# Inner products of two token blocks at a time, and gate products in halves of the array, in a fused mLSTM and feed-forward kernel

## The chip, the cores and the metric

The kernel runs on one core of a Trainium2 chip. The metric is the device time of one execution in microseconds; before the change three runs took 475.63, 476.14 and 476.31 us, so the median is 476.14. The core has five engines with a queue of instructions each, which run in order and wait for one another by semaphores: TensorE (PE in the rows; PEld are its weight loads), VectorE (DVE), ScalarE (ACT), GpSimd (POOL) and SyncE (SP), which issues the DMAs.

## The reference

Three parts follow each other. First an mLSTM with a stabilised exponential gate, over 768 steps for 2 batches and 8 heads of 40 channels:

```python
m_new = np.maximum(f_gate[:, :, t] + m, i_gate[:, :, t])
f_stab = np.exp(f_gate[:, :, t] + m - m_new)
i_stab = np.exp(i_gate[:, :, t] - m_new)
C = f_stab[:, :, None, None] * C + i_stab[:, :, None, None] * np.einsum('bhd,bhe->bhde', vt, kt)
n = f_stab[:, :, None] * n + i_stab[:, :, None] * kt
h_tilde = np.einsum('bhde,bhe->bhd', C, qt)
denom = np.maximum(np.abs(nq), 1.0)
y[:, :, t] = o * h_tilde / denom
```

Its 1536 tokens of 320 channels go through a feed-forward part with 2048 inner columns and a rational function, and then through a gated one with 1536 inner columns:

```python
h = x @ w_in
P = a[0] + a[1] * h + a[2] * h2 + a[3] * h3
Q = 1.0 + np.abs(b[0]) * np.abs(h) + np.abs(b[1]) * h2
g = P / (Q + 1e-06)
x = g @ w_out
...
xn = x / rms * rms_g
silu = g * (1.0 / (1.0 + np.exp(-g)))      # g = xn @ w_gate
return (silu * val @ w_out)                # val = xn @ w_val
```

The weights come as 64-bit floats and are converted on the chip. Most products are made of 32-bit parts with a high and a low half, three products for one.

## The kernel before, in words

**Attention.** The sequence is cut into 12 chunks of 128 steps (6 for each batch). For chunk j TensorE makes the scores `s` (line 506), the forget gates' products `f` (line 486), the outputs from the state `yi` (530) and from the chunk `y` (547), and the state's update `u` (559). `f` spreads a row of gates over 128 partitions: for each head one product of a 48 x 128 selection (weights) with 128 steps; a scan on VectorE (489) turns it into decays, with which the scores are multiplied (511). `y` and `yi` are already made in halves of 64 array columns. The scan, the update and the output have steps on VectorE, GpSimd and ScalarE. The outputs of a chunk are transposed on TensorE (`xt`, 652) and split into a high part (`xh`, ScalarE, 656) and a low part (`xl`, VectorE, 660) in the tile `xall`.

**First feed-forward part.** The tokens are cut into 6 blocks of 256 (two chunks each), the inner columns into 8 pairs of 256. A unit i is one block and one pair: `PAIRS[i]` is (block, pair). Blocks 0 and 1 alternate over the pairs (units 0 to 15); then each of blocks 2 to 5 goes through all 8 pairs (units 16 to 47). A unit's inner products are tasks `in0` and `in1` (line 683): for each of two groups of 128 inner columns 8 products that move 256 tokens, into one bank of PSUM of 128 x 512. Then comes the rational function, on 128 x 512 elements: `hu`, `z`, `p1`, `h2` and `ars`, `sq` on ScalarE; `zu`, and `p2` in even units, on GpSimd; `p2` in odd units, `p3`, `w`, `y2`, `g` on VectorE (727 to 746). `g` gives the result, and tasks `out0` and `out1` multiply it by `w_out` into the accumulators of its block: units 0 to 15 in full 32-bit products (line 688), later ones in high and low parts (702, 704).

**Weights.** `c0`, `c1` (VectorE, 335 to 347), `cr`, `hi` (ScalarE) and `c2` and the last split (GpSimd, 360, 368) convert a block of weights. In0 of unit i waits for its pair of weights and for the `xl` of its block.

**Second feed-forward part.** The blocks' results are scaled, stored, loaded and transposed again; the gated products (872) and the output products (880 to 882) follow on TensorE. They fill the time from about 300 us to the end alone.

**What sets the order.** Every piece of work is a task with a number, made by `task(...)`. The table ORDER lists all 1946 numbers; `run()` (called at the end) goes through it and issues each task's instructions, and takes and gives back buffers by name (`b` are the 8 banks of PSUM). The order of instructions on each engine is thus the order in the table. These lines fix the units and the wait of the inner products:

```python
PAIRS = [(n, x - n * LAG) for x in range(NPAIR + LAG) for n in range(2) if 0 <= x - n * LAG < NPAIR]
PAIRS += [(n, p) for n in range(2, NB) for p in range(NPAIR)]
...
go("in0", lambda: inp(0), [("i", p), ("coefs",)] + ([("out0", i - 6)] if i >= 6 else []) + [("xl", 2 * n + t) for t in range(2)], ["h"])
```

## Time and profile before

| | |
|---|---|
| median of 3 runs | 476.14 us (475.63 to 476.31) |
| the profiled execution | 475.63 us, its span 473.9 us |
| TensorE busy | 457.1 us, 96% of the span, 3712 instructions |
| VectorE, ScalarE, GpSimd busy | 324.5, 307.2 and 312.2 us |
| chain that ended last | TensorE 67%, GpSimd 11%, VectorE 9%, ScalarE 8% |
| inner products, line 683 | 768 of 128 x 256, busy 104.1 us |
| forget gates' products, line 486 | 96 of 128 x 128, busy 10.1 us |

Busy times of TensorE count records whose ends are modelled: products overlap in the array, and what one costs is read from the distance between starts. The chain that ended last is followed back from the last instruction, at each step to what released it. A product of full 32-bit operands is recorded as two.

### The profile page before, as it was taken

What the parts mean: (1) busy time and instruction counts of PE and PEld (TensorE: products, weight loads), DVE (VectorE), ACT (ScalarE), POOL (GpSimd) and SP (SyncE); (2) the same over time, 40 slices, a digit from 0 to 9 for tenths busy, and PEclk for the clock granted to TensorE, in tenths of its full rate; (3) what the DMA queues carried; (4) which work ended last, traced back from release to release, by engine and by line L of the source; (5) the groups of instructions that cost most, each with busy time, mean ns of one, the idle gap of its engine ahead of it and who ended that gap; (6) DMA issues with size and microseconds to landing.
All of it is one profiled execution on the core that took longest, in us unless ns stands there. A gap on an engine that the chain in (4) does not pass through costs nothing.

```text
span 473.9 us, 9691 instructions
## 1 busy us (share of the span) xinstructions
PE 457.1 (96%) x3712; PEld 417.0 (88%) x3712; DVE 324.5 (68%) x610; ACT 307.2 (65%) x578; POOL 312.2 (66%) x326
## 2 busy tenths in 40 slices
PE   5799899999999999999999999999999999999997
PEld 4697887787889999999899888988988889999996
DVE  7899999999899999999999998972222111102201
ACT  2437999899999999999999999543131321222221
POOL 3699999999888998797797767975221431211250
PEclk9999999999999999999999999999999999999999
DMA  8797633250050104102114247422000010010001
GB/s 239 220 304 185 187 141 100 97 143 8 1 150 17 48 16 118 60 27 84 57 55 142 65 132 234 141 86 92 25 14 28 26 36 1 1 57 0 15 2 57
DMA packets 18367, 40.42 MB, mean 85 GB/s; under 512 B 3952, under 2 KB 11904, under 8 KB 18320
## 3 DMA queue, kind: packets, MB, share of 16 engines
q1 hardware_dynamic: 18320, 39.80, 27.2%
q8 instruction: 29, 0.48, 0.4%
q14 instruction: 18, 0.15, 0.1%
HBM read 35.86 MB, written 3.93 MB: 84 GB/s over the span
## 4 chain that ended last, share of the span: by engine, by line
PE 67%; POOL 11%; DVE 9%; ACT 8%; issue 3%; DMA 1%; DVEq 0%; POOLq 0%; ACTq 0%
PE bank L872 28%; PE bank L683 10%; PE bank L702 7%; PE bank L882 4%; PE bank L881 4%; PE bank L880 4%; PE bank L704 3%; POOL z L727 2%; DVE w_buf L489 2%; POOL win L368 2%; POOL vv L729 1%; POOL cv L360 1%; POOL wou L368 1%; ACT bank L739 1%; PE bank L547 1%
## 5 line engine op out<-in xcount | busy, mean ns | idle before, releaser
L683 PE MATMUL bank<-xall,win 128*128 128x256 f32 x768 | 104.1, 289 | 2.4 <-DVE xall L660 0.7
L683 PEld LDWEIGHTS bank<-xall,win 128*128 128x128 f32 x768 | 97.0, 193 | 6.6 <-DVE xall L660 1.1
L948 DVE TENSOR_TENSOR vv<-bank,vv 128x512 f32<-128x512 f32 x35 | 23.7, 688 | 69.9 <-PE bank L872 61.1
L727 POOL TENSOR_TENSOR z<-z,u 128x512 f32<-128x512 f32 x48 | 61.9, 1291 | 10.0 <-ACT z L717 9.5
L954 POOL TENSOR_TENSOR wou<-vv,wou 128x512 fp32r<-128x512 f32 x18 | 23.2, 1295 | 55.2 <-ACT wou L951 49.5
L945 ACT ACTIVATE vv<-bank 128x512 f32<-128x512 f32 x35 | 20.7, 595 | 55.1 <-PE bank L872 47.8
L756 POOL TENSOR_TENSOR gl<-vv,gh 128x512 fp32r<-128x512 f32 x32 | 41.3, 1295 | 12.9 <-issue 5.9
L872 PE MATMUL bank<-xall,w2gv 128*128 128x512 f32 (+1 forms) x256 | 46.3, 337 | 0.0
L872 PEld LDWEIGHTS bank<-xall,w2gv 128*128 128x128 f32 x256 | 39.0, 190 | 4.5
L717 ACT ACTIVATE z<-u,few 128x512 f32<-128x512 f32 x48 | 39.0, 813 | 1.0
L702 PE MATMUL bank<-wou,gh 128*128 128x320 f32 x128 | 38.6, 314 | 0.0
L704 PE MATMUL bank<-wou,gh 128*128 128x320 f32 x128 | 38.0, 309 | 0.0
L688 PE MATMUL bank<-scr,vv 128*128 128x320 f32 x128 | 37.4, 437 | 0.0
L742 DVE SCALAR_TENSOR_TENSOR z<-z,bank 128x512 f32<-128x512 f32 x48 | 32.8, 682 | 4.9 <-ACT bank L741 3.8
L335 DVE TENSOR_SCALAR bank<-raw 128x320 int32<-128x320 int32 x68 | 32.6, 487 | 4.8 <-DMA raw<-in_w_out_dram 4.2
L744 DVE SCALAR_TENSOR_TENSOR bank<-vv,few,bank 128x512 f32<-128x512 f32 x48 | 35.8, 747 | 0.0
L739 ACT ACTIVATE bank<-z,few 128x512 f32<-128x512 f32 x48 | 32.9, 685 | 2.6 <-POOL z L727 2.0
L746 DVE SCALAR_TENSOR_TENSOR vv<-z,bank 128x512 f32<-128x512 f32 x48 | 32.5, 681 | 0.7
L872 PE MATMUL bank<-win,w2gv 128*128 128x512 f32 x128 | 30.8, 391 | 0.0
L688 PEld LDWEIGHTS bank<-scr,vv 128*128 128x128 f32 x128 | 23.2, 190 | 8.4 <-issue 0.2
L716 ACT ACTIVATE u<-bank 128x512 f32<-128x512 f32 x48 | 28.5, 594 | 2.6 <-POOL z L727 1.0
L368 POOL TENSOR_TENSOR win<-cv,win 64x128 fp32r<-64x128 f32 (+2 forms) x37 | 28.0, 756 | 3.1 <-ACT win L364 1.2
(169 smaller groups left out, 1170.1 us busy)
## 6 DMA issues: line engine op xcount, KB each, us to landing
raw<-in_w_out_dram SPq DMA_DIRECT2D x14, 640.0 KB, 4.0
raw<-in_w_gv_dram SPq DMA_DIRECT2D x12, 640.0 KB, 4.1
raw<-in_w_in_dram SPq DMA_DIRECT2D x8, 640.0 KB, 5.7
lqk<-in_qk_tr_dram SPq DMA_DIRECT2D x24, 192.0 KB, 5.0
lv<-in_v_dram SPq DMA_DIRECT2D x12, 160.0 KB, 5.0
los<-in_o_gate_dram SPq DMA_DIRECT2D x12, 160.0 KB, 5.8
lk<-in_k_dram SPq DMA_DIRECT2D x12, 160.0 KB, 3.9
z_dram<-rnd SPq DMA_DIRECT2D x6, 320.0 KB, 2.3
```

What stands on the lines that cost most here:

```text
L368: POOL.tensor_tensor(out=lo, in0=v, in1=r32(hi), op=ALU.subtract)
L683: PE.matmul(out=hb()[:, e], lhsT=l, rhs=r, start=(x == 0), stop=(x == len(mm) - 1))
L688: PE.matmul(out=T("acc", n, t)[:, 0:DM], lhsT=T("vv", i)[:, e, t * 128:(t + 1) * 128], rhs=w[:, e], start=p + e == 0, stop=p == NPAIR - 1 ...
L702: PE.matmul(out=o, lhsT=l, rhs=woh[:, e], start=first, stop=last)
L704: PE.matmul(out=o, lhsT=l, rhs=wol[:, e], start=False, stop=False)
L717: go("z", lambda: ACT.activation(out=z(), in_=u(), func=ACTF.Identity, scale=babs[:, 1:2], bias=babs[:, 0:1]), [("hu", i)], ["z"])
L727: go("zu", lambda: POOL.tensor_tensor(out=z(), in0=z(), in1=u(), op=ALU.mult), [("z", i)], [], ["u"])
L739: go("ars", lambda: ACT.activation(out=hb(), in_=z(), func=ACTF.Abs_reciprocal_sqrt, bias=cq), [("zu", i), ("p3", i)])
L742: go("w", lambda: DVE.scalar_tensor_tensor(out=z(), in0=z(), scalar=1.0 + 1e-6, in1=hb(), op0=ALU.add, op1=ALU.mult), [("sq", i)])
L744: go("y2", lambda: DVE.scalar_tensor_tensor(out=hb(), in0=vv(), scalar=nacoef[:, 0:1], in1=hb(), op0=ALU.add, op1=ALU.mult), [("w", i)])
L756: go("gl", lambda: POOL.tensor_tensor(out=gl(), in0=vv(), in1=r32(gh()), op=ALU.subtract), [("gh", i)], ["gl"], ["vv"])
L872: PE.matmul(out=bank(i, e), lhsT=l, rhs=r, start=y == 0, stop=y == len(mm) - 1)
```

## The change

`NARROW = [2, 8, 8]` replaces LAG: for blocks 0 and 1 the first two pairs stay as they were (units 0 to 3). From the third pair on a unit is one group of 128 inner columns for both blocks, 512 tokens: units 4 to 15 are such wide units. Their inner products move 2 x 256 tokens in one product, so a unit has 8 products and not 16 (`in0` the first 4, `in1` the last 4), in the same bank; the polynomial has the same shapes; `out0` serves one block, `out1` the other. `in0` of a wide unit waits for the `xl` of both blocks. Blocks 2 to 5 keep their units. The forget gates' products are made as two products of 64 array columns each. ORDER is another list of the same 1946 numbers.

```diff
@@ -20,102 +20,102 @@
 OB = [["ob"] * 4, ["raw", "raw", "raw", "ob"], ["ob", "raw"], ["ob", "cv"]]
 F_CV = [1] * 16 + [0] * 18
 NATIVE = [0, 1, 2, 3, 4, 5, 6, 7, 8, 9, 10, 11, 12, 13, 14, 15]
-LAG = 0
+NARROW = [2, 8, 8]
 BY_SQUARE = [0, 2, 4, 6, 8, 10, 12, 14, 16, 18, 20, 22, 24, 26, 28]
 ORDER = [
-    0, 8, 9, 10, 18, 34, 372, 11, 12, 373, 374, 375, 3, 2, 14, 39, 40, 41, 4, 16, 43, 44, 1, 13, 15, 60, 65, 66, 410,
...
+    0, 8, 34, 9, 18, 10, 11, 372, 3, 377, 373, 12, 2, 14, 375, 37, 38, 374, 16, 39, 40, 41, 43, 44, 60, 1, 13, 17, 19,
...
 ]
...
@@ -163,9 +163,15 @@
 
     BLOCKS = [(0, 2 * BLK), (2 * BLK, 2 * BLK), (4 * BLK, BLK), (5 * BLK, BLK)]
 
-    PAIRS = [(n, x - n * LAG) for x in range(NPAIR + LAG) for n in range(2) if 0 <= x - n * LAG < NPAIR]
-    PAIRS += [(n, p) for n in range(2, NB) for p in range(NPAIR)]
-    FINAL = [max(i for i, x in enumerate(PAIRS) if x[0] == n) for n in range(NB)]
+    UNITS = []
+    for n, few_ps in zip(range(0, NB, 2), NARROW):
+        narrow = [(m, p) for m in (n, n + 1) for p in range(few_ps)]
+        if n == 0:
+            narrow = [(m, p) for p in range(few_ps) for m in (n, n + 1)]
+        UNITS += [([m], [2 * p, 2 * p + 1]) for m, p in narrow]
+        both = [n, n + 1] if n % 3 < 2 else [n + 1, n]
+        UNITS += [(both, [f]) for f in range(2 * few_ps, 2 * NPAIR)]
+    FINAL = [max(i for i, x in enumerate(UNITS) if n in x[0]) for n in range(NB)]
 
     PE, ACT, DVE, POOL = nc.tensor, nc.scalar, nc.vector, nc.gpsimd
 
@@ -236,7 +242,7 @@
         return [wou[:, x * 2 * DM:(x + 1) * 2 * DM].rearrange("p (f d) -> p f d", d=DM) for x in (2 * p, 2 * p + 1)]
 
     def words_of(p):
-        return [i for i, x in enumerate(PAIRS) if x[1] == p and i in NATIVE]
+        return [i for i, x in enumerate(UNITS) if x[1][0] // 2 == p and i in NATIVE]
 
     ring("raw", tiles(w1, 3, [128, 1280], I32, "raw"))
     ring("rnd", tiles(w1, 2, [128, 640], I32, "rnd"))
@@ -483,7 +489,8 @@
             t = four(T("pf", j, g))
             for e in range(4):
                 bh = b * H + 2 * e + g
-                PE.matmul(out=t[:, e], lhsT=sel[:, bh:bh + 1].to_broadcast([48, 128]), rhs=f16[:, cut])
+                for c in (slice(0, 64), slice(64, 128)):
+                    PE.matmul(out=t[c, e], lhsT=sel[:, bh:bh + 1].to_broadcast([48, 64]), rhs=f16[:, cut])
 
         def scan(g):
             DVE.tensor_tensor_scan(
@@ -663,45 +670,49 @@
     last_of = {}
 
     def pair(i):
-        n, p = PAIRS[i]
-        xt = xts[n % 3]
+        ns, fs = UNITS[i]
+        p = fs[0] // 2
+        wide = len(ns) == 2
+        slots = [n % 3 for n in ns]
+        xt = xall.rearrange("p h a (x t) -> p h a x t", x=3)[:, :, :, slots[0]:slots[-1] + 1:max(1, slots[-1] - slots[0])]
+        cells = [(n, t, f) for f in fs for n in ns for t in range(2)]
 
         def hb():
             return T("h", i).rearrange("p (e t) -> p e t", e=2)
 
         def inp(e):
-            c0 = (2 * p + e) * 128
+            c = slice(fs[0 if wide else e] * 128, fs[0 if wide else e] * 128 + 128)
             mm = []
             for a in range(2):
-                mm += [
-                    (whi[:, a, c0:c0 + 128], xt[:, 0, a]),
-                    (whi[:, a, c0:c0 + 128], xt[:, 1, a]),
-                    (wli[:, a, c0:c0 + 128], xt[:, 0, a]),
-                ]
-            mm += [(wre[:, c0:c0 + 128], xt[:, 0, 2]), (wre[:, c0:c0 + 128], xt[:, 1, 2])]
-            for x, (l, r) in enumerate(mm):
-                PE.matmul(out=hb()[:, e], lhsT=l, rhs=r, start=(x == 0), stop=(x == len(mm) - 1))
+                mm += [(whi[:, a, c], 0, a), (whi[:, a, c], 1, a), (wli[:, a, c], 0, a)]
+            mm += [(wre[:, c], 0, 2), (wre[:, c], 1, 2)]
+            for x, (l, y, a) in enumerate(mm):
+                if not wide:
+                    PE.matmul(out=hb()[:, e], lhsT=l, rhs=xt[:, y, a, 0], start=x == 0, stop=x == len(mm) - 1)
+                elif x // 4 == e:
+                    PE.matmul(out=hb(), lhsT=l, rhs=xt[:, y, a], start=x == 0, stop=x == len(mm) - 1)
 
         def whole(e):
-            for t in range(2):
-                w = T("co", "o", p).rearrange("p (f d) -> p f d", d=DM)
-                PE.matmul(
-                    out=T("acc", n, t)[:, 0:DM], lhsT=T("vv", i)[:, e, t * 128:(t + 1) * 128], rhs=w[:, e],
-                    start=p + e == 0, stop=p == NPAIR - 1 and e == 1,
-                )
+            w = T("co", "o", p).rearrange("p (f d) -> p f d", d=DM)
+            for x, (n, t, f) in enumerate(cells):
+                if x // 2 == e:
+                    PE.matmul(
+                        out=T("acc", n, t)[:, 0:DM], lhsT=flat(T("vv", i))[:, x * L:(x + 1) * L], rhs=w[:, f % 2],
+                        start=f == 0, stop=f == 2 * NPAIR - 1,
+                    )
+
+        def flat(t):
+            return t.rearrange("p a b -> p (a b)")
 
         def outp(low):
             woh, wol = wout(p)
-            gp = T("gl" if low else "gh", i)
-            for e in range(2):
-                f = 2 * p + e
-                first, last = f == 0 and not low, f == DFF // 128 - 1 and low
-                for t in range(2):
-                    o = T("acc", n, t)[:, 0:DM]
-                    l = gp[:, e, t * 128:(t + 1) * 128]
-                    PE.matmul(out=o, lhsT=l, rhs=woh[:, e], start=first, stop=last)
-                    if not low:
-                        PE.matmul(out=o, lhsT=l, rhs=wol[:, e], start=False, stop=False)
+            gp = flat(T("gl" if low else "gh", i))
+            for x, (n, t, f) in enumerate(cells):
+                o = T("acc", n, t)[:, 0:DM]
+                l = gp[:, x * L:(x + 1) * L]
+                PE.matmul(out=o, lhsT=l, rhs=woh[:, f % 2], start=f == 0 and not low, stop=f == 2 * NPAIR - 1 and low)
+                if not low:
+                    PE.matmul(out=o, lhsT=l, rhs=wol[:, f % 2], start=False, stop=False)
 
         def go(nm, fn, deps, take=(), give=()):
 
@@ -711,7 +722,7 @@
             task((nm, i), fn, deps + after, take, [(x, i) for x in give])
 
         u, z, vv, hh, gh, gl = (lambda nm=nm: T(nm, i) for nm in ("u", "z", "vv", "s", "gh", "gl"))
-        go("in0", lambda: inp(0), [("i", p), ("coefs",)] + ([("out0", i - 6)] if i >= 6 else []) + [("xl", 2 * n + t) for t in range(2)], ["h"])
+        go("in0", lambda: inp(0), [("i", p), ("coefs",)] + ([("out0", i - 6)] if i >= 6 else []) + [("xl", 2 * n + t) for n in ns for t in range(2)], ["h"])
         go("in1", lambda: inp(1), [("in0", i)])
         go("hu", lambda: ACT.activation(out=u(), in_=hb(), func=ACTF.Abs), [("in1", i)], ["u"])
         go("z", lambda: ACT.activation(
@@ -747,7 +758,7 @@
             out=vv(), in0=z(), scalar=2.0, in1=hb(), op0=ALU.subtract, op1=ALU.mult), [("y2", i)],
             [], ["z", "h"])
         ready = [("w", "o", p) if i in NATIVE else ("o", p)] + ([("out1", i - 1)] if i else [])
-        accs = [("b", ("acc", n, t)) for t in range(2)] if p == 0 else []
+        accs = [("b", ("acc", n, t)) for n in ns for t in range(2)] if fs[0] == 0 else []
         if i in NATIVE:
             task(("out0", i), lambda: whole(0), [("g", i)] + ready, accs)
             go("out1", lambda: whole(1), [("out0", i)], [], ["vv"])
```

**TensorE, the first units.** Before, behind chunk 5's gate products: unit 3's inner products, unit 0's output products (`vv_94` is its result), and the inner products of units 4 and 5. The other names are banks of PSUM, `xall` and the inner weights `win`:

```order
L683 MATMUL bank_70<-xall,win 128x256 x16
L688 MATMUL bank_69<-scr,vv_94 128x320
L688 MATMUL bank_72<-scr,vv_94 128x320
L688 MATMUL bank_69<-scr,vv_94 128x320
L688 MATMUL bank_72<-scr,vv_94 128x320
L683 MATMUL bank_75<-xall,win 128x256 x8
L683 MATMUL bank_73<-xall,win 128x256 x8
L683 MATMUL bank_75<-xall,win 128x256 x8
L683 MATMUL bank_73<-xall,win 128x256 x8
```

And the same place after, where line 691 makes narrow products (here units 2 and 3) and line 693 wide ones:

```order
L691 MATMUL bank_70<-xall,win 128x256 x8
L693 MATMUL bank_72<-xall,win 128x512 x8
L691 MATMUL bank_73<-xall,win 128x256 x8
L693 MATMUL bank_71<-xall,win 128x512 x4
L699 MATMUL bank_69<-scr,vv_94 128x320
L699 MATMUL bank_76<-scr,vv_94 128x320
L693 MATMUL bank_74<-xall,win 128x512 x4
L699 MATMUL bank_69<-scr,vv_94 128x320
L699 MATMUL bank_76<-scr,vv_94 128x320
L693 MATMUL bank_71<-xall,win 128x512 x4
L693 MATMUL bank_74<-xall,win 128x512 x4
```

Units 0 to 3 have products of 256 as before; units 4 and later have 4 + 4 of 512, and those of unit 4 and half of unit 5 now stand ahead of unit 0's output products.

**TensorE, unit 15.** Before: the last two output products of unit 14's first block, the state's update of chunk 6 (line 559), unit 15's output products (`vv_97`), inner products and the scores of chunk 7:

```order
L688 MATMUL bank_69<-scr,vv_96 128x320
L688 MATMUL bank_72<-scr,vv_96 128x320
L559 MATMUL bank_75<-v_buf,lk_122 64x41 x8
L688 MATMUL bank_71<-scr,vv_97 128x320
L688 MATMUL bank_74<-scr,vv_97 128x320
L683 MATMUL bank_76<-xall,win 128x256 x16
L506 MATMUL bank_75<-lqk_124 128x128
L506 MATMUL bank_69<-lqk_124 128x128
```

After (output products are line 699, scores 513, the update 566):

```order
L699 MATMUL bank_70<-scr,vv_97 128x320
L699 MATMUL bank_75<-scr,vv_97 128x320
L513 MATMUL bank_71<-lqk_123 128x128
L513 MATMUL bank_73<-lqk_123 128x128
L513 MATMUL bank_71<-lqk_123 128x128
L513 MATMUL bank_73<-lqk_123 128x128
L513 MATMUL bank_71<-lqk_123 128x128
L513 MATMUL bank_73<-lqk_123 128x128
L513 MATMUL bank_71<-lqk_123 128x128
L513 MATMUL bank_73<-lqk_123 128x128
L691 MATMUL bank_74<-xall,win 128x256 x16
L566 MATMUL bank_69<-v_buf,lk_122 64x41 x8
```

The update of chunk 6 moved behind unit 15's output products and the scores of chunk 7.

**VectorE, the end of unit 15's polynomial.** Before, from unit 14's `w` (742) to unit 15's `g` (746 into `vv_97`):

```order
L742 SCALAR_TENSOR_TENSOR z_93<-z_93,bank_75 128x512
L744 SCALAR_TENSOR_TENSOR bank_75<-vv_96,few,bank_75 128x512
L746 SCALAR_TENSOR_TENSOR vv_96<-z_93,bank_75 128x512
L742 SCALAR_TENSOR_TENSOR z_91<-z_91,bank_76 128x512
L744 SCALAR_TENSOR_TENSOR bank_76<-vv_97,few,bank_76 128x512
L578 RECIPROCAL den<-den 128x8
L746 SCALAR_TENSOR_TENSOR vv_97<-z_91,bank_76 128x512
```

After (lines are 11 higher; `vv_94` is now unit 16's):

```order
L753 SCALAR_TENSOR_TENSOR z_93<-z_93,bank_71 128x512
L755 SCALAR_TENSOR_TENSOR bank_71<-vv_96,few,bank_71 128x512
L757 SCALAR_TENSOR_TENSOR vv_96<-z_93,bank_71 128x512
L742 SCALAR_TENSOR_TENSOR vv_94<-bank_74,few,vv_94 128x512
L753 SCALAR_TENSOR_TENSOR z_91<-z_91,bank_73 128x512
L755 SCALAR_TENSOR_TENSOR bank_73<-vv_97,few,bank_73 128x512
L757 SCALAR_TENSOR_TENSOR vv_97<-z_91,bank_73 128x512
```

The third step of unit 16 (line 742 of the changed kernel) now stands ahead of unit 15's `g`, and the reciprocal of chunk 6 behind it.

## Rows read from the trace of the kernel before

**Rows 1.** Windows: from:to, length, busy time (instructions) of each engine, clock, DMA.
```profile
38.80:60.00 21.20, 18.73 (x214) 16.59 (x211) 20.26 (x40) 18.90 (x35) 20.34 (x24) 1.00 0.63 182
60.00:132.00 72.00, 70.66 (x535) 57.67 (x535) 67.68 (x120) 68.07 (x124) 68.89 (x71) 1.00 0.25 76
132.00:228.00 96.00, 95.63 (x1060) 91.00 (x1059) 91.45 (x162) 91.39 (x172) 82.59 (x88) 1.00 0.21 64
228.00:252.00 24.00, 23.33 (x174) 22.30 (x172) 23.06 (x45) 23.67 (x51) 21.11 (x21) 1.00 0.25 82
```

**Rows 2.** The chain that ended last: start, length, engine, tile, line.
```profile
57.24 1.23 POOL z L727
...
133.34 4.09 PE bank L683 x32
...
210.93 3.83 PE bank L683 x32
...
242.47 2.17 PE bank L683 x16
...
313.85 10.90 PE bank L872 x48
```

**Rows 3.** Line 683, the inner products: durations, and who waited for them.
```profile
L683 PEld LDWEIGHTS bank<-xall,win x768: 186/192/333, 38.9 to 268.9; 128*128 128x128 f32 x192
L683 PE MATMUL bank<-xall,win x768: 274/283/582, 38.9 to 269.1; 128*128 128x256 f32 x192
...
who waited for it (us, times):
  ACT u L716: 0.9, 2
```

**Rows 4.** TensorE's timeline at unit 15's output product: start, length, count.
```profile
126.20 0.67 PE L559 MATMUL bank<-v_buf,lk 128*64 128x41 f32 x16
126.80 1.34 PE L688 MATMUL bank<-scr,vv 128*128 128x320 f32 x4
```

**Rows 5.** VectorE's timeline at the end of unit 15's polynomial.
```profile
125.43 0.20 DVE L578 RECIPROCAL den<-den 128x8 f32<-128x8 f32 x1 [0.34 <-POOL den L576]
125.55 0.64 DVE L746 SCALAR_TENSOR_TENSOR vv<-z,bank 128x512 f32<-128x512 f32 x1
...
126.77 0.75 DVE L731 SCALAR_TENSOR_TENSOR vv<-bank,few,vv 128x512 f32<-128x512 f32 x1
```

**Rows 6.** TensorE's timeline at chunk 8.
```profile
135.83 1.60 PE L683 MATMUL bank<-xall,win 128*128 128x256 f32 x12
137.36 0.68 PE L530 MATMUL bank<-cst,lqk 40*64 40x41 f32 x32
137.96 1.13 PE L547 MATMUL bank<-vp_buf,scr 128*64 128x41 f32 x32
139.03 1.16 PE L506 MATMUL bank<-lqk 40*128 40x128 f32 x16
140.02 0.61 PE L486 MATMUL bank<-f,sel 48*128 48x128 f16 x8
140.56 2.17 PE L683 MATMUL bank<-xall,win 128*128 128x256 f32 x16
```

**Rows 7.** Line 486, the forget gates' products: durations min/median/max in ns.
```profile
L486 PEld LDWEIGHTS <-sel x96: 92/96/148, 7.5 to 195.2; 48*128 48x128 f16 x96
L486 PE MATMUL bank<-f,sel x96: 213/216/311, 7.5 to 195.2; 48*128 48x128 f16 x96
```

**Rows 8.** VectorE's timeline at the first four transposed chunks.
```profile
42.57 0.49 DVE L341 SCALAR_TENSOR_TENSOR scr<-raw,bank 128x320 int32<-128x320 int32 x1
...
45.79 1.00 DVE L660 TENSOR_TENSOR xall<-bank,xall 128x384 fp32r<-128x384 f32 x2
46.70 0.68 DVE L511 TENSOR_TENSOR scr<-bank,w_buf 128x512 f32<-128x512 f32 x1
...
49.34 0.32 DVE L568 TENSOR_TENSOR cst<-bank,cst 128x164 f32<-128x164 f32 x1
```

184 rows, old and new, of the table ORDER are left out of this document.

## The prediction

> **What bounds the kernel now.** I read the windows of the span first, then the chain of work that ended last, then the lines and the timelines of single places. The windows show a kernel with hardly any free engine: from 60 to 132 us TensorE is busy 70.66 of 72.00 us, VectorE 67.68, ScalarE 68.07 and GpSimd 68.89; from 132 to 228 us TensorE has 95.63 of 96.00 and VectorE and ScalarE 91 each [rows 1]. Two numbers tell more than these shares. The first is where the chain lies: from about 38 us it runs over GpSimd, ScalarE and VectorE (the piece at 57.24 is one of many of that kind), and it comes to TensorE with the products at 133.34; from there TensorE carries it to the end, but for a stretch on ScalarE and VectorE that ends with the products at 242.47 [rows 2]. So before 133 us the polynomial of the first feed-forward part and the weights' conversion set the pace, and after it TensorE's own work does. The second is what a TensorE record means: a 256-column product has a record of 283 ns [rows 3], but 32 of them take 3.83 us, 119.7 ns each [rows 2]. A stall shorter than 160 ns thus leaves no idle time in the windows, and what a product costs is read from its spacing alone.
>
> **The change part by part.** All durations come from the profiled execution, which took 475.63 us (a span of 473.9 and 1.7 around it); the median of the three runs, 476.14, lies 0.51 above it. I sum differences and put them on the median.
>
> *The wide units.* Twelve units (4 to 15) change from 16 products of 256 columns to 8 of 512. By spacing, 16 x 119.7 ns = 1.92 us; 48 products of 512 columns in the gated part take 10.90 us, 227.1 ns each, and 8 of them 1.82 us [rows 2]. That is 0.10 us a unit and 1.2 us in all. Their output products keep their count, and the polynomial's instructions keep their shapes. All twelve stand ahead of unit 15's output product, which starts at 126.80 [rows 4], before the chain comes to TensorE. What hides the saving is the work of GpSimd, ScalarE and VectorE; were that cover gone, the full 1.2 us would come through. Between these ends (0 and -1.2) I take -0.3: the polynomials' first step sat idle for these products for 0.9 us in two waits, all told [rows 3], and a shorter product can shorten no more than that.
>
> *The trace on the spacing, and a rule.* Two products of 256 columns cost 2 x 119.7 = 239.4 ns, one of 512 costs 227.1: 12.3 ns less a pair, on 96 pairs 1.2 us [rows 2]. The Trainium skill (TensorE: Matmul & The Clock Gate, Back-to-back issue gap) gives an isolated warm product N / 2.4 + 2.5 ns; my estimate by that page is 2.5 ns a pair, 0.24 us in all instead of 1.2, and the sum below would be higher by 0.2. The trace does not agree with it for this stream, whose weights are 32-bit and change with each product.
>
> *Up to unit 15.* I compared what stands on each engine ahead of unit 15's last steps. VectorE has one instruction more, the third step of unit 16 (0.75 us as in the row at 126.77), and one less, a reciprocal of 0.20 [rows 5]: +0.55 us. GpSimd has one scaling of the values more. Before, unit 15's last step ended at 125.55 + 0.64 = 126.19 [rows 5], and its product came at 126.80, because TensorE did chunk 6's state update between, 16 products in 0.60 us [rows 4]. In the new order the update is moved behind the product and the next chunk's scores. The product can then follow its polynomial at once, at 126.19 + 0.55 = 126.74: the same time to 0.1 us. But the update is still to be done, on TensorE and now where TensorE carries the chain: +0.6. Bounds: -0.6 (the three other engines close their gaps, 3 to 4 us each in this window [rows 1]) and +0.75 more.
>
> *Changes of array shape.* The attention products use parts of the array (40 rows, or 64 columns), the others all of it. At chunk 8, 12 products of 256 columns from 135.83 should end by spacing at 137.27, and the next kind starts at 137.36: 0.09 us [rows 6]. In the other direction 8 gate products at 56 ns (their records: 0.61 us less the last one's 216 ns, over 7) should end at 140.47, and the next kind starts at 140.56: 0.09 again [rows 6, 7]. Counted in the two orders behind unit 15's product, such changes are 39 before and 49 now. Four of the ten come from the gates themselves: scores and gates had one shape and now have two. No row shows that pair, so it costs between 0 and 0.09; I take 0 for the four and 0.09 for the six: +0.54 (up to +0.9).
>
> *The gates' halves.* 96 products of 128 array columns become 192 of 64, two of which can run in both halves of the array at once. A pair still moves 128 columns, so it can't take less than the 56 ns of the single product. Line 547 has the same form, 32 instructions or 16 pairs in 1.07 us at chunk 8, 66 ns a pair [rows 6]. From chunk 7 on there are 40 pairs: 0 to +0.4 us when side by side, +2.2 when each half waits for the other (2 x 56 ns). I take +0.2. The earlier chunks' gates lie where VectorE sets the pace.
>
> *A rule against the halves.* A 128-column load of 16-bit weights takes 92 to 96 ns, one of 32-bit weights 192 [rows 3, 7]. The Trainium skill (TensorE: Matmul & The Clock Gate, Weight-path perf modes) says why: the fast load needs 128 weights and a type that is not FP32. The halves have 64 weights and would lose it; by the same page's LDWEIGHTS rule a half takes 53 ns, an estimate, and two in turn 107. The trace agrees on the two kinds of whole load; of a 16-bit half it shows nothing.
>
> *The stretch before 242 us.* From 228 to 252 us TensorE is idle 0.67 us [rows 1], at two waits for VectorE, and the chain leaves TensorE there [rows 2]. In the new order unit 41's 16 inner products stand ahead of unit 36's output products, so TensorE has 1.9 us more in hand when it comes there. I take this wait as gone, -0.67 (bounds -1.0 with the 0.37 of the window before, and 0).
>
> *Sum:* -0.3 + 0.6 + 0.54 + 0.2 - 0.67 = +0.4 us: 475.63 becomes 476.0, and the median 476.14 becomes **476.5 us**. A measurement of this kernel can tell about 0.2%, 0.95 us, from no change: my forecast is no change.
>
> **The rivals.**
>
> *A: the saving passes to the end, faster.* Speaking for it: TensorE is the fullest engine in every window, and the others have gaps of 3 to 4 us before 132 us [rows 1], which another order can close. Against it: nothing in the order gives these three engines less to do ahead of unit 15. Then -1.2 stands in place of -0.3, the update is covered (0), the waits of 1.0 go: -1.2 + 0.54 + 0.2 - 1.0 = -1.5, so 474.6 us. By the page's spacing it would be 475.6.
>
> *B: the start comes later, slower.* The mechanism is in the first four chunks: the last transposed part of x was ready on VectorE at 45.79 + 1.00 = 46.79. In the new order four more VectorE instructions stand ahead of it: chunk 4's two products with the decays (0.68 each), a conversion (0.49) and a state update (0.32), 2.2 us [rows 8], and GpSimd has a weight split and two attention steps more ahead of its own part. The second token block's first products wait for this, and VectorE was busy 20.26 of 21.20 us there [rows 1], so it can't catch up. For it: these engines carry the chain there. Against it: the instructions are moved, not added, and by unit 3 VectorE has done the same set. Price: 2.2 us, 478.3. It decides if that last transposed part ends later than 49 us and unit 3's output product, too, is 2 us late.
>
> *C: the halves run in turn.* 40 pairs at 56 ns more after unit 15 instead of 0.2: +2.0, 478.5 us. For it: the halves share their rows of the array and lose the fast load. Against it: line 547's halves overlap.
>
> **How the numbers follow.** Forecast 0.44, A 0.27, B 0.2, C 0.09. The forecast's own range is 475.3 to 477.7; its upper part is slower by over 0.2%, a tenth of it. So within 0.2%: 0.39; A and a small part of the forecast faster: 0.28; B, C and the forecast's upper part slower: 0.33. The range that leaves out 2 in 10 goes from 473.9 (A with the switches at half price) to 479.0 (B with the switches at full price).
>
> **What would show it.** In the changed profile: products of 512 columns on xall and win at 227 ns (else the first term falls); unit 15's output product within 0.7 us of 126.8, with the chain not on TensorE before it (earlier by over 1 us: A); the last transposed part of the first four at 47 to 49 us (later: B); groups of 16 gate halves in 0.5 to 0.6 us (0.9: C); 0.09 us lost at each change of shape, and none or as much from scores to gates; less than 0.3 us of idle TensorE from 228 to 252 us. The forecast is wrong if the time leaves 475.2 to 477.1.

## The result: slower by 4.6 us, and the profile after

The changed kernel takes 480.83 us (median of 4 runs, 480.64 to 481.09) against 476.23 (475.63 to 476.4): a ratio of 1.0102, 95% interval 1.0090 to 1.0114. The forecast was 476.5, no change. Its profiled execution took 481.09 us, its span 479.3.

The windows of after with the cuts of [rows 1], and one more; columns as there:

```profile
38.80:60.00 21.20, 21.20 (x267) 19.02 (x266) 19.06 (x39) 16.92 (x33) 19.11 (x27) 1.00 0.62 191
60.00:132.00 72.00, 69.11 (x410) 49.87 (x408) 68.52 (x120) 67.63 (x118) 68.32 (x66) 1.00 0.28 85
132.00:228.00 96.00, 95.72 (x1112) 90.35 (x1112) 89.49 (x160) 88.05 (x174) 79.91 (x86) 1.00 0.18 52
228.00:252.00 24.00, 23.24 (x177) 22.74 (x176) 23.57 (x44) 23.55 (x46) 19.55 (x20) 1.00 0.33 102
228.00:262.00 34.00, 33.03 (x249) 31.91 (x248) 33.26 (x62) 33.42 (x68) 28.09 (x28) 1.00 0.24 73
```

Two changes matter. In the first window TensorE has no idle time left (it was busy 18.73 of 21.20 us before), while ScalarE and VectorE do 2.0 and 1.2 us less. From 132 to 228 us TensorE is as full as before, but ScalarE does 88.05 us of work instead of 91.39: 3.3 us are left for later. VectorE and GpSimd do less there too (89.49 for 91.45, 79.91 for 82.59). From 228 to 262 us ScalarE is busy 33.42 of 34.00 us in either kernel.

The clock column counts as 1.00 all that lies ahead of the trace's first record of the clock, which stands at 49.4 us here and at 41.5 us before. The level ahead of it is read from the spacing: in the chain below, 32 output products of the attention (L554) take 1.86 us at 32.72 us and 1.06 us at 140.24.

The chain that ended last in after (start, length, what), in the start, at two later places and from 240 us:

```profile
15.95 4.01 DMA los<-in_o_gate_dram
19.96 0.64 PE bank L473 x2
...
32.72 1.86 PE bank L554 x32
...
45.58 3.41 PE bank L691 x16
...
117.14 1.20 PE bank L693 x4
...
140.24 1.06 PE bank L554 x32
...
240.66 0.70 ACT z L728
241.35 0.72 ACT w2gv L370 x2
242.09 0.31 ACT w2gv L370
242.41 0.63 ACT gh L766
243.03 0.59 ACT bank L750
```

It runs on TensorE without a break from 19.96 to 54.6 us. Before, it was on GpSimd, ScalarE and VectorE from 38 us on [rows 2]. It also comes back to TensorE at 117.14 us, sooner than before (133.34), and leaves it once more at unit 15. And from 228 to 262 us its pieces add up to 19.1 us on ScalarE, 6.4 on GpSimd and 6.8 on TensorE; before, they were 5.8 on ScalarE, 5.7 on VectorE and 19.7 on TensorE. There the chain lies on ScalarE for the most part, no longer on TensorE.

The places that the prediction named, on TensorE and VectorE (start, length, line, tiles, shape, count):

```profile
98.79 2.11 PE L693 MATMUL bank<-xall,win 128*128 128x512 f32 x8
...
133.22 2.18 PE L691 MATMUL bank<-xall,win 128*128 128x256 f32 x16
135.33 0.67 PE L566 MATMUL bank<-v_buf,lk 128*64 128x41 f32 x16
135.93 0.63 PE L493 MATMUL bank<-f,sel 48*64 48x128 f16 x16
136.50 3.14 PE L691 MATMUL bank<-xall,win 128*128 128x256 f32 x24
```

```profile
51.31 0.56 DVE L667 TENSOR_TENSOR xall<-bank,xall 128x384 fp32r<-128x384 f32 x1 [0.58 <-ACT xall L663]
128.73 0.69 DVE L757 SCALAR_TENSOR_TENSOR vv<-z,bank 128x512 f32<-128x512 f32 x1
```

```profile
L493 PEld LDWEIGHTS <-sel x192: 102/107/174, 7.7 to 205.1; 48*64 48x64 f16 x192
L493 PE MATMUL bank<-f,sel x192: 216/239/313, 7.7 to 205.1; 48*64 48x128 f16 x192
```

Unit 15's last step on VectorE starts at 128.73, 3.2 us later than the 125.55 of [rows 5]. The last of the first four transposed parts ends at 51.87 instead of 46.79 [rows 8]. Sixteen gate halves take 0.57 us to the next kind. Chunk 6's state update (L566 at 135.33) now lies behind unit 15's product.

That step stands in every kernel here, so I measure each by two numbers: when it starts, and what passes from there to the end of the span. Before: 125.55 and 473.9 - 125.55 = 348.4. After: 128.73 and 350.6. So 3.2 us were lost ahead of it and 2.2 behind it. Together that is 5.4 us and not 4.6, because each kernel has one profiled execution, and before's was the lowest of its runs and after's the highest. In the three kernels of the table below that keep before's order without extra products it starts at 126.13 to 126.26 us, so some 0.6 us of the 3.2 belong to that one execution. Another 0.55 us is work of VectorE that the new order puts ahead of the step, by the prediction's own count.

### The profile page after: what moved, and what is told of

Read it like the earlier page. It is cut to its first block, busy times and chain, and to the rows that moved or that the text cites. A ratio compares the mean times of both kernels' runs of the same rounds, so it can differ in the third digit from the quotient of the medians.

```text
span 479.3 us, 9665 instructions
## 1 busy us (share of the span) xinstructions
PE 461.3 (96%) x3712; PEld 413.5 (86%) x3712; DVE 327.7 (68%) x610; ACT 306.4 (64%) x578; POOL 312.1 (65%) x326
## 4 chain that ended last, share of the span: by engine, by line
PE 73%; ACT 12%; POOL 8%; DMA 3%; issue 2%; DVE 1%; SPq 1%; POOLq 0%; ACTq 0%; DVEq 0%
PE bank L883 28%; PE bank L691 11%; PE bank L713 6%; PE bank L892 4%; PE bank L893 4%; PE bank L891 4%; PE bank L715 3%; PE bank L513 3%; DMA raw<-in_w_in_dram 3%; POOL z L738 2%; ACT z L728 2%; PE bank L554 2%; ACT u L727 2%; PE bank L659 2%; PE bank L566 1%
## 5 line engine op out<-in xcount | busy, mean ns | idle before, releaser
L691 PE MATMUL bank<-xall,win 128*128 128x256 f32 x576 | 78.0, 290 | 0.7 <-ACT xall L663 0.4
L691 PEld LDWEIGHTS bank<-xall,win 128*128 128x128 f32 x576 | 73.4, 195 | 2.4 <-ACT z L728 0.6
L965 POOL TENSOR_TENSOR gl<-vv,wou 128x512 fp32r<-128x512 f32 x9 | 11.6, 1292 | 39.4 <-ACT wou L962 39.4
L965 POOL TENSOR_TENSOR wou<-vv,gh 128x512 fp32r<-128x512 f32 x9 | 11.6, 1292 | 37.2 <-ACT gh L962 37.1
L965 POOL TENSOR_TENSOR wou<-vv,wou 128x512 fp32r<-128x512 f32 x13 | 16.8, 1294 | 21.1 <-ACT wou L962 21.0
```

Of the source, the lines that this page charges most:

```text
L691: PE.matmul(out=hb()[:, e], lhsT=l, rhs=xt[:, y, a, 0], start=x == 0, stop=x == len(mm) - 1)
L965: task(("sl",) + k2, lambda: POOL.tensor_tensor(out=flat("sl", *k2), in0=flat("sg", *k2), in1=r32(flat("sh", *k2)), op=ALU.subtract), [("s ...
```

## The experiments

All times are against runs of the kernel before on the same chip (475.96 to 476.23 us in the medians). "Unit 15" and "behind" are the two numbers just defined, from the profiled execution of each. Three theories stood at first: the start is the loss (1, with 1a the late loads and 1b the clock), the changes of array shape are (2), or the wide units. Where an expectation gives 2 or 3 a new sense, it says so.

| kernel | us | against before | ratio, 95% | unit 15 | behind |
|---|---|---|---|---|---|
| before (profile) | 475.63 | | | 125.55 | 348.4 |
| after | 480.83 | +4.6 | 1.0090 to 1.0114 | 128.73 | 350.6 |
| b_wide | 477.49 | +1.5 | 1.0021 to 1.0046 | 126.23 | 349.5 |
| b_halves | 476.58 | +0.6 | 1.0002 to 1.0020 | 126.26 | 348.6 |
| a_order | 480.21 | +4.3 | 1.0077 to 1.0104 | 127.60 | 350.8 |
| a_wide | 480.28 | +4.1 | 1.0070 to 1.0102 | 127.40 | 350.9 |
| a_dma | 480.51 | +4.6 | 1.0080 to 1.0107 | 127.30 | 350.6 |
| start_a2 | 477.47 | +1.3 | 1.0016 to 1.0036 | 126.97 | 348.3 |
| start_b2 | 480.10 | +3.9 | 1.0065 to 1.0092 | 127.64 | 351.2 |
| late_b | 479.03 | +3.0 | 1.0046 to 1.0070 | 126.58 | 351.0 |
| a_hi3 | 479.81 | +3.8 | 1.0067 to 1.0097 | 127.39 | 350.7 |
| a_hi3v2 | 479.86 | +3.8 | 1.0062 to 1.0088 | 127.70 | 350.7 |
| a_swap | 480.45 | +4.4 | 1.0080 to 1.0106 | 127.38 | 351.1 |
| b_swap | 476.27 | +0.2 | 0.9995 to 1.0012 | 126.13 | 348.6 |
| b_warm2 | 477.22 | +1.0 | 1.0007 to 1.0025 | 127.21 | 348.6 |

### The three parts of the change, each alone

b_wide has before's order, with the wide units (`NARROW = [2, 8, 8]`) and whole gate products; the first block's normalization had to wait for unit 15's first product instead of unit 14's last:

```diff
-        task(("rms0", n), squares, [("out1", FINAL[n]), ("ld", "rg")] + ([("rmsa", n - 1)] if n else []),
+        task(("rms0", n), squares, [("out1" if n else "out0", FINAL[n]), ("ld", "rg")] + ([("rmsa", n - 1)] if n else []),
```

> The order of before and whole gate products; only the units change: from the third pair on, 128 inner columns for 512 tokens. Theory 1 (the new order's start-up costs about 3 us, the units nothing): no loss here, 475.0 to 476.4 us, with the first full-array inner products near 38.9 us as before. Rival (a 512-token unit has to wait for both halves of its input, so the units themselves are the loss): 478 us or more, with TensorE waiting in front of unit 4 or the units behind it. By the spacing of the products alone (1.2 us less on TensorE) it can't be under 474.9.

b_halves has before's order and `NARROW = [8, 8, 8]`, and only the gates are halved:

```diff
-                PE.matmul(out=t[:, e], lhsT=sel[:, bh:bh + 1].to_broadcast([48, 128]), rhs=f16[:, cut])
+                for c in (slice(0, 64), slice(64, 128)):
+                    PE.matmul(out=t[c, e], lhsT=sel[:, bh:bh + 1].to_broadcast([48, 64]), rhs=f16[:, cut])
```

> The order of before and its 256-token units; only the forget gates' products change, from one of 128 array columns to two of 64. Theory 2 (eight changes of array shape from scores to gates at 0.096 us, 0.8 us, and a pair of halves at the old spacing): 476.8 to 477.2 us. Theory 1 (all of the loss is the start-up): 476.2, no change. If the halves were the loss: 480.

a_order has after's `ORDER` with `NARROW = [8, 8, 8]` and whole gates; a_wide has after's `ORDER` and units, with whole gates:

```diff
-NARROW = [2, 8, 8]
+NARROW = [8, 8, 8]
```

> The order of after, with the 256-token units and the whole gate products of before. Theory 1: the loss is in the order, 479.5 to 480.5 us (less only the eight changes of shape, 0.8 us, and more by the 256-token spacing where it is not hidden). Rival (units and gates make the loss, the order none): 476 to 477.

> The order of after with its 512-token units, and the whole gate products of before. Against the run with the order alone (480.2) it prices the wide units in this order: 0 to -1.2 us by my forecast's term, so 479.0 to 480.2; against the kernel after (480.8) it prices the gate halves there: 0.8 us by the eight changes of shape, so 480.0. If the units' later end of the first block costs here what it did in the order of before (1.1 us): 481.3.

The order alone makes 4.3 of the 4.6 us. The wide units change nothing in it that these runs can tell (a_wide against a_order: +0.07 in the medians, with intervals 1.3 and 1.5 us wide). The halves cost 0.6 us in the order of before (b_halves, 0.1 to 1.0) and 0.5 in that of after (after against a_wide), which the intervals there don't tell from nothing. In the order of before the wide units do lose, 1.5 us, and the trace of b_wide shows where: between the last steps of units 15 and 16 on VectorE it falls back by 1.2 us against before, and hardly anywhere else. A wide unit holds both blocks, so the first block's sums are complete only with unit 15. ScalarE's squares wait for them, and TensorE's scores then wait for the bank that the normalization frees (ScalarE, then TensorE, start, length, and the wait in brackets):

```profile
128.31 0.44 ACT L785 ACTIVATE rnd<-bank 128x320 f32<-128x320 f32 x1 [0.96 <-PE bank L698]
```

```profile
131.67 1.04 PE L512 MATMUL bank<-lqk 40*128 40x128 f32 x13 [0.34 <-ACT rnd L799]
```

### Where the order loses: ahead of unit 15 or behind it

a_dma is after with the loads of the halves table and of the identity put forward on SyncE's queue, right behind `("ld", "eye4")`.

> The kernel after, with two loads moved forward on SyncE's queue: the halves table and the identity, right behind the four-fold identity. Theory 1a (the late loads are the start-up's loss, since TensorE waits 2.6 and 2.1 us for them before 20 us): 478 to 479 us, and the first full-array inner products 2 to 3 us earlier than 45.2. Theory 1b (the loss is the work of chunks 1 to 3 that stands ahead of those products, and with them the later rise of the granted clock): 480.5, no change, the waits only move to the next load.

The first full-array inner products start at 44.3 us instead of 45.2 (a_order and a_wide, with the loads of after, have 44.6 and 44.4), and the time is that of after: theory 1a falls. TensorE's wait of 2.12 us up to 19.95 us stays as long, now for VectorE instead of the load.

start_b and start_a cut the two orders at unit 1's second products and join them crosswise. In both the joint itself made a new wait.

> Units and gates of before; the order of before up to unit 1's second output products (the first 59 us), and behind them the order of after. If the loss is the new order's start alone: 476, no change, and no lag at unit 3's output product. If the later part of the new order loses by its moved state update and its changes of array shape: 476.9 to 478.5 us, with the loss between 130 and 300 us. Together with the run of after's start this should add up to the 4.2 us that the whole order lost.

> Units and gates of before; the order of after up to unit 1's second output products (the first 64 us), and behind them the order of before. Theory 1 (the start is the loss, and GpSimd, ScalarE and VectorE carry it from unit 3 to unit 15 without regaining it): unit 3's output product and unit 15's both about 2 us late, 477.7 to 478.5 us. Rival (the start's delay is taken up before 133 us, and the rest of the order makes the loss): 476.

start_b took 480.09 us and start_a 490.67. SyncE's queue in start_b (start, length, load): a load of v (`lv`), put early, waits until 65.35 us for its buffer, which GpSimd frees, and the sixth weight (`in_w_in`) is issued behind it, at 66.20 instead of 54.22 before. In start_a a wait of the same sort holds the queue from 52.0 to 72.9 us.

```profile
55.36 1.36 SPq L295 DMA_DIRECT2D lk<-in_k_dram  x1
65.35 0.33 SPq L295 DMA_DIRECT2D lv<-in_v_dram  x1
65.73 0.42 SPq L295 DMA_DIRECT2D los<-in_o_gate_dram  x1
66.20 0.42 SPq L329 DMA_DIRECT2D raw<-in_w_in_dram  x1
```

Neither says anything about the start. start_b2 and start_a2 are the same without that wait: four loads of start_b moved behind `("ld", "i", 6)`, three of start_a further back.

> As the run before with the start of before and the rest of after, but four loads of the attention that stood ahead of the sixth weight's load on SyncE (there the queue waited from 56 to 65 us for a buffer, and VectorE then 1.2 us for that weight) now stand behind it. Theory 1 (the start costs some 2 us and the later part 2.4): unit 15's output product within 0.8 us of 126.8, and 478.0 to 478.8 us. Rival (the new order's work from 60 to 130 us is the slower, whatever the start): unit 15 at 128.3 again, and 480.

> As the run before with the start of after and the rest of before, but two loads of the attention for which SyncE's queue waited 20 us there now stand where the order of after has them. Theory 1: unit 3's and unit 15's output products 1.5 to 2.5 us late, and 477.7 to 478.5 us. Rival (the delay is taken up before 133 us): 476.2.

The start of after costs 1.3 us by itself (start_a2), and nothing behind unit 15 (348.3). The rest of after's order costs 3.9, so the two are not a sum: in start_b2 unit 15 comes as late as in a_order. So from 60 to 130 us the new order has a loss of its own, which covers the start's. late_b keeps before's order up to unit 13 and takes after's behind it:

> Units and gates of before; the order of before up to unit 13's first step (117 us), and behind it that of after. What is left is the loss behind unit 13: the moved state update (0.6), seven waits of TensorE instead of three (3.4 us against 1.5 in the two traces) and six changes of array shape (0.3 to 0.5 us), together 2.4 us by the two traces: 478.2 to 478.8. If the later part loses only because the earlier is late: 476.2.

3.0 us, nearly all of it behind unit 15 (351.0). So 1.3 us ahead of 117 us and 3.0 behind make up a_order's 4.3. late_c was to cut again at unit 35:

> Units and gates of before; the order of before up to the first step of unit 35 (some 221 us), and behind it that of after. Of the 3.0 us that the order of after loses behind 117 us, this keeps only the waits behind 221 us: 476.4 to 476.9 us. The other 2.2 to 2.6 us then lie between 117 and 221 us, with the moved state update and most of the changes of array shape. If the loss lay in the stretch of the second part's start alone: 478.5.

It took 479.97 us (+3.9), but its joint made two waits of its own at 217.3 and 218.7 us (1.05 and 0.69 us of idle TensorE), so it doesn't tell where the 3.0 lie.

### Single waits

a_hi3 puts one rounding of ScalarE ahead, for which GpSimd waited at 95.3 us; a_hi3v2 also puts GpSimd's scaling of chunk 6's values back.

> The order of after with the units and gates of before (480.2 us), and one instruction moved: ScalarE's rounding of the upper parts of the fourth output weight stands three weight and unit steps earlier, as GpSimd waits 0.88 us for it at 95.3 us. Theory 2 (GpSimd sets the pace from 60 to 130 us, and its waits there are the loss): its rest of that weight 0.8 us earlier, unit 15's output product at 127.7 to 128.0 instead of 128.6, and 479.3 to 479.6 us. Rival (the start's delay on TensorE and VectorE decides): 480.2, no change.

> The same, and GpSimd's scaling of chunk 6's values (0.75 us) goes back behind unit 15's first step, where it stood before. Theory 2: unit 15's output product another 0.3 to 0.7 us earlier, 478.7 to 479.3 us. If the wait and the scaling cost nothing at the end: 480.2.

GpSimd's waits from 60 to 132 us in a_order and in a_hi3 (engine, line, who; us in total, times, longest):

```profile
POOL z L737 <- ACT z L727: 1.3, 5, 0.3
POOL wou L374 <- ACT wou L370: 0.9, 1, 0.9
```

```profile
POOL z L737 <- ACT z L727: 1.6, 5, 0.5
POOL vv L739 <- ACT vv L730: 0.2, 1, 0.2
```

The wait of 0.9 us is gone, 0.5 of it came back in front of the next steps, and the median moved by 0.4 us, which the intervals (1.3 and 1.4 us wide) don't tell from nothing; the scaling added nothing (479.86). Both expectations of a gain were missed. a_swap and b_swap aim in the same way at TensorE's waits behind 130 us, four and two of them. One change of a_swap, on VectorE (a step of a weight's conversion goes ahead of the third normalization):

```diff
+L353 SCALAR_TENSOR_TENSOR cv_88<-raw_83,bank_71 128x320
 L793 TENSOR_TENSOR bank_73<-bank_73,few 128x2
 L794 TENSOR_SCALAR bank_73<-bank_73 128x2
 L795 TENSOR_TENSOR few<-bank_73,few 128x2
-L353 SCALAR_TENSOR_TENSOR cv_88<-raw_83,bank_71 128x320
```

> The order of after with the units and gates of before (480.2 us), and four instructions of VectorE and ScalarE changed over with a neighbour, so that what TensorE waits for at 217.7, 235.0, 241.6 and 255.5 us (0.42, 0.55, 0.52 and 0.39 us beyond the spacing) comes first; TensorE's own order stays. Theory 3 (behind 130 us TensorE carries the chain, and each of its waits passes to the end one for one): 478.3 to 479.0 us. Rival (TensorE only waits elsewhere, since VectorE and ScalarE are the later ones): 480.0 to 480.4.

> The kernel before with two such changes, both on VectorE: chunk 7's first scan one step earlier (TensorE waits 0.53 us at 132.7 us for the bank that it frees), and the last step of a weight's conversion one step earlier (0.54 us at 235.9). Theory 3: 0.7 to 1.1 us less, 475.0 to 475.4 us against 476.1. Rival: no change.

The gain of theory 3 did not come: 480.45 and 476.27 us. The waits were moved more than taken away. In a_swap the idle time of TensorE ahead of 242.22 us in a_order (0.36 us) is gone, but that at 235.7 us grew from 0.39 to 0.57 and that at 256.0 from 0.22 to 0.39. TensorE's idle times in b_swap from 228 to 262 us:

```profile
232.05 2.06 PE L690 MATMUL bank<-xall,win 128*128 128x256 f32 x15 [0.21 <-DVE xall L666]
242.95 2.17 PE L690 MATMUL bank<-xall,win 128*128 128x256 f32 x16 [0.45 <-DVE cv L353]
```

The two waits of before that were aimed at are gone, and a new one of 0.45 us has come at 242.95. The chain of b_swap from 228 to 290 us has 17.8 us on ScalarE, where before had 5.8: with TensorE's wait moved, the chain goes over ScalarE, which is busy 33.4 of 34 us there. That is nearly as much as in after (19.1), and b_swap loses nothing; where the chain lies is thus no measure of a loss.

### The clock in the start

b_warm, b_warm2 and a_warm add full-array products of a tile of ones, in before's and after's kernel:

```diff
+        DVE.memset(rings["vv"][3].rearrange("p a b -> p (a b)"), 1.0)
...
+            task(("wm", x), lambda: PE.matmul(
+                out=rings["b"][0][:, 0:256], lhsT=wm[:, 0:128], rhs=wm[:, 0:256], start=True, stop=True))
```

(b_warm and a_warm took a bank of their own for each.)

> The kernel before, with 8 more full-array products (128x128 by 256 columns, whole 32-bit words, on a tile of ones; nobody reads the result) where TensorE waits in the first 16 us: 4 ahead of the first scores, 1 and 2 ahead of the gates' transpositions, 1 ahead of the first output of the attention. Theory 1b (the granted clock stands at 1.2 GHz until TensorE has done full-array products, and the start runs at that level up to 41.5 us): the attention products of the first chunks have 56 ns a gate product instead of 107 from about 10 us on, the first full-array inner products come 1 to 3 us earlier than 38.9, and the kernel takes 473.5 to 475.5 us. If the clock falls back during the attention products, or the other engines set the start: 476, no change.

> The kernel after with 10 such products: 4 ahead of the first scores, 3 ahead of the first gates' transpositions, 1 ahead of the first output of the attention, 2 ahead of the decays. In this kernel TensorE alone carries the chain from 20 to 54 us, at 1.2 GHz up to 49.4 us. Theory 1b: at 2.4 GHz from about 10 us on that stretch shortens by some 5 us or more, the first full-array inner products come before 41 us, and the kernel takes 476.5 to 478.5 us. If only the work ahead of those products counts and the clock doesn't: 480.8, no change.

> As the first run with extra full-array products in the kernel before, but they write to the bank that the next attention product takes anyway, so that the rotation of the banks stays as it was (in the first run the scores came to a bank that VectorE had just used, and waited 3.6 us for it). Theory 1b: the granted clock rises before 20 us, falls back to 1.2 GHz while TensorE does the attention's products alone, and the time is 475.0 to 476.2 us. If it stays up: 473.5 to 475. If nothing rises: 476, no change.

They took 480.68, 484.82 and 477.22 us. In b_warm the shifted rotation of the banks gave the scores a bank that VectorE had just used:

```profile
9.51 1.86 PE L513 MATMUL bank<-lqk 40*128 40x128 f32 x13 [3.57 <-DVE cv L347]
```

All behind it came some 4.5 us late, and so did the end: a start that is late on every engine passes through whole. In the profiled execution of b_warm2 the level didn't rise before 44 us: 32 output products of the attention took 1.93 us there up to 38 us, against 1.13 at chunk 8 [rows 6]. Ten of its twelve runs have a mean granted clock of 0.960 to 0.964, the other two 0.999 and 1.000. So in the ten there must have been an early rise and some 34 us at the low level behind it (an estimate: 0.036 of 475.8 us, at half the clock), as a_warm's trace has it: up at 5.2 us, down from 8.6 to 53.0. The ten took 476.75 to 477.71 us, all more than before's median of 476.19. Theory 1b's gain isn't borne out, and extra products only cost time.

## Why the prediction was wrong, by its own steps

Two steps failed, "up to unit 15" and "the stretch before 242 us", and the term for the changes of shape was too small. The measured 480.83 us lies above the range (up to 479.0) and above every rival's time (478.5 at most). The terms one by one:

*The wide units (-0.3):* measured 0.0, within what their end of the range allowed. At the same six places, 16 narrow products of a_order take 1.99 to 2.25 us to the next kind and eight wide ones of a_wide 1.90 to 2.18, 0.06 to 0.12 less each; the saving is there, and hidden. The rule on the spacing thus decided nothing.

*Up to unit 15 ("the same time to 0.1 us") failed.* I compared the work ahead of unit 15's last step on each engine, found 0.55 us more, and took equal work for equal time. What I left out is the order inside the start: TensorE's chain from 19.96 to 54.6 us. There the order of after does one more chunk's scores and gates, one more state update and one more chunk's transposition ahead of the first inner products (45.2 us; 38.9 in [rows 3]), and TensorE works at half its clock up to then. Rival B named this place, and by its own test it held: 51.87 us for the transposed part (over 49), and unit 3 3.5 us late. Alone it costs 1.3 us (start_a2), not 2.2. My argument against it, that by unit 3 VectorE has done the same set, is beside the point. Nor is the start all of it: with before's start and the rest of after (start_b2) unit 15 comes as late.

*Chunk 6's update (+0.6):* at 135.33, 0.6 us to the next kind, as forecast.

*Changes of shape (+0.54):* I summed in both traces what each product takes beyond the usual spacing of its kind. At changes of shape it is 4.4 us before (42 of them behind unit 15's product, the four from scores to gates among them, those with a wait aside) and 5.4 after (47): +1.0. From scores to gates, which I took at 0, the halves add 0.10 each.

*The halves (+0.2):* 16 in 0.57 us, side by side, so C is out; with the changes of shape, 0.5 to 0.6 (b_halves; after against a_wide). *The rule against the halves:* the load of a half takes 107 ns [L493 above], more than the 96 of a whole one. My estimate of 53 ns was by the Trainium skill (TensorE: Matmul & The Clock Gate, LDWEIGHTS); the trace does not agree with it. By the Trainium skill (TensorE: Matmul & The Clock Gate, Weight-path perf modes) a load of 64 weights isn't a fast one; a record that got longer agrees. Sixteen loads of 107 ns stand in those 0.57 us, so they overlap, and the longer load isn't seen in the sum.

*The stretch before 242 us (-0.67) failed, and most of all.* The idle time from 228 to 252 us is 0.76 us (0.67 before). By the same sum over spacings, TensorE's waits (over 0.25 us beyond the spacing) behind unit 15's product are 2.6 us after and 1.5 before: +1.1 in place of -0.67. I had read from the order that TensorE has more in hand at one wait. But in a_swap and b_swap the end did not move when single waits were moved, so the wait that I took away on paper was no price by itself. What the windows show besides is ScalarE's share: 3.3 us less done from 132 to 228 us, while TensorE was just as full. Every kernel of the table with that order behind unit 15 shows it (87.7 to 88.1 us, against 91.0 to 91.4 with the order of before), and every one takes 350.6 to 351.2 us behind unit 15, against 348.3 to 348.6 (b_wide 349.5). The window of late_b, and of start_a2 with before's order there (ScalarE is the fourth of the busy times):

```profile
132.00:228.00 96.00, 95.47 (x1067) 90.36 (x1066) 89.52 (x159) 87.80 (x170) 81.39 (x86) 1.00 0.19 56
132.00:228.00 96.00, 95.60 (x1064) 90.67 (x1062) 91.35 (x162) 91.32 (x173) 82.77 (x86) 1.00 0.21 61
```

The four terms behind unit 15's product thus came to 1.1 (waits) + 1.0 (shapes) + 0.45 (the update without its changes of shape) - 0.1 (gates' own) = 2.5 us in the trace of after, where I had +0.67. From that product to the end the traces have 349.6 us after (from 129.73) and 347.1 before (from 126.80), 2.5 more. This says where TensorE's time went, not which engine made it wait.

What stays open: that the work which ScalarE is left with is the cause of the 2.2 to 2.9 us, and the waits only its sign, is read from windows and not shown. VectorE and GpSimd are left with more as well, b_swap's chain lies on ScalarE at no loss, and no run here relieved ScalarE alone. The moved update and the changes of shape were not put back one by one in after's order either. Nor is it settled which instruction makes the loss of 0.9 us from 60 to 117 us (3.9 of start_b2 less 3.0 of late_b) that covers the start's. No kernel tried beats the kernel before.

## What to carry to other kernels

Equal work ahead of a milestone is not equal time: in a new order, follow the chain through the start first, at the clock that holds there. Where three engines are over 90% busy, a wait read from one of them is no price: when it is taken away at one place it can come back at the next, so ask which engine has more work left behind the place. And two orders can be cut and joined to find where one loses, if the loads and waits in the joint are looked at first.

## What was not expected of the hardware

TensorE's granted clock stayed at 1.2 GHz through 20 us in which TensorE was never idle. It did mostly the attention's products there, which use part of the array (40 rows, or 64 columns), and from 38.87 us on the first inner products, which use all of it. The windows of b_swap (the clock, in parts of 2.4 GHz, stands behind the busy time of the last engine):

```profile
19.40:22.70 3.30, 1.96 (x48) 1.62 (x47) 3.27 (x9) 2.76 (x4) 0.70 (x4) 1.00 0.23 56
23.00:43.00 20.00, 20.00 (x252) 18.07 (x254) 19.12 (x45) 8.46 (x22) 18.70 (x29) 0.50 0.89 262
44.00:60.00 16.00, 13.76 (x177) 11.92 (x173) 15.47 (x27) 15.05 (x27) 14.90 (x16) 1.00 0.54 142
```

In b_swap it had risen once, at 19.4 us, and fell at 22.8, behind a stretch in which TensorE was busy 1.96 of 3.30 us. It rose for good 1 to 5 us behind the first full-array inner products (by the trace's record of the clock at 41.5 us in before, 49.4 in after) in every kernel but start_a: there it fell once more, at 78.3 us, while TensorE stood idle from 76.1 to 85.9 us. The Trainium skill (TensorE: Matmul & The Clock Gate, Part 1: The HAM clock gate) says that the clock is throttled by default and that activity releases it. The row at 23 us, busy 20.00 of 20.00 us at a granted clock of 0.50, does not agree with that. At one and the same start the rise came between 41.5 and 43.5 us, and unit 0's last step on VectorE came 0.3 to 1.0 us later in the other kernels with that start than in the profile of before.
